# The denominator's product of a rational layer, on GpSimd from two magnitudes of ScalarE in place of VectorE from PSUM

## The chip, the core and the metric

The kernel runs on one core of one Trainium2 chip. The metric is the device time of one execution in microseconds, lower is better; the kernel before takes 723.6 us (median of three runs). A core has five engines that run their own instruction lists in order and wait for each other through semaphores: PE (TensorE, matrix products into PSUM), DVE (VectorE), ACT (ScalarE), POOL (GpSimd, which here reads and writes SBUF alone) and SP (which issues the DMAs).

## What is computed

Three stages follow each other. Attention with pooled queries gives `x` (1152 tokens by 512). The first layer puts a rational function between two matrix products, and the second layer is a gated one:

```python
h = x @ w_in                                  # 1152 x 2048
P = a[0] + a[1] * h + a[2] * h * h + a[3] * h * h * h
Q = 1.0 + np.abs(b[0]) * np.abs(h) + np.abs(b[1]) * h * h
g = P / (Q + 1e-06)
x = g @ w_out
...
silu = g * (1.0 / (1.0 + np.exp(-g)))         # second layer, g = xn @ w_gate
out = silu * (xn @ w_val) @ w_out
```

Only the first layer is touched. With u = |h|, the part of Q beyond 1 is (|b0| + |b1| u) u.

## The kernel before

Each product of the two layers is made from three passes (high by high, low by high, high by low part of the operands), so a block of 128 by 384 by 128 costs three matmuls. The 2048 hidden columns of the first layer are 16 **units** of 128; a unit's tile is 128 by 1152, in three parts of 384 tokens (`c`). PE makes a unit's `hid` tile (36 matmuls, lines 485 to 551) in one of two PSUM buffers. Units 0 and 1 are worked part by part (384 columns an instruction), the others whole (1152).

`rational` (line 1070) makes g from `hid`, and its steps are the names used below, with the unit behind them (p3_5 is p3 of unit 5):

- abs (L1106, ACT): `m_u` = |b1 h| from PSUM. p1 (L1109, ACT): `m_p` from PSUM. p2 (L1112, DVE) and p3 (L1115, DVE): the numerator's polynomial, each reads `m_p` and `hid`. p3 is the last to read `hid`, so it frees the PSUM buffer for the unit after next.
- q (L1122, DVE): `m_q` = (|b1 h| + |b0|) h, from `m_u` and PSUM. aq (L1125, ACT): its magnitude, which is the denominator's product.
- ln (L1128) and exp (L1134), ACT: the reciprocal of 1 + product, in `m_u`.
- One Newton step: q1 (L1131, ACT) and M (L1140, POOL) in even units, M (L1137, DVE) in odd ones.
- t (L1143, DVE), g (L1146, DVE): the quotient; both read SBUF alone. hi (L1154, ACT) and lo (L1157, POOL): its high and low part, which PE multiplies with `w_out`.

There are two buffers each of `m_u` and `m_q`, three of `m_p`, seven of `g_hi` and `g_lo`. `out1` (line 1193) sums g @ w_out over groups of units (0-1, 2-5, 6-9, 10-13, 14-15) in one of two PSUM buffers `accp`, and adds each finished block into `acc`: on ACT for the first group (L1210), on DVE for the others (L1212). Late in the layer the three instructions that turn a raw weight into fp32 (L176, L180, L186, DVE) and its split (L199, L204) stand between these steps.

What sets the order: every step is an `Op` with an engine, a cost by a formula (`cost`, line 428), a key and its buffers, and `order` (line 331) writes the engines' lists from these by a list schedule at build time. The costs know nothing of one engine that slows another. On the chip the lists are fixed, and every engine takes its own in order.

Of the kernel before, what the change touches and what calls it, by code (L numbers as in the profile page):

```python
# [11 lines left out]
AF = mybir.ActivationFunctionType  # L12
# [7 lines left out]
def attention_moe_moe2_kernel(  # L20
# [18 lines left out]
    nc = tc.nc  # L39
# [67 lines left out]
    b0, b1 = absb[:, 0:1], absb[:, 1:2]  # L107
# [204 lines left out]
            self.last = None  # L312

    ON_POOL = range(0, 16, 2)
    TOLL = {"DVE": 1.5, "ACT": 1.5}

    busy = {}
# [13 lines left out]
    def order(slack):  # L331
# [8 lines left out]
        def start(op):  # L340
# [5 lines left out]
            for way in op.ways:  # L346
                op.eng, op.cost, op.fn = way
                t = begin(op)
                w = t + op.cost * TOLL.get(op.eng, 1.0)
                if best is None or w < best[0]:  # L350
# [4 lines left out]
        def begin(op):  # L355
            e = op.eng
            if e not in op.data:
                op.data[e] = max((d.end + handoff(d.eng, e) for d in op.deps), default=0.0)
            t = max(busy.get(e, 0.0), op.data[e])
            if e == PE and op.mode != mode[0]:  # L360
                t = max(t, busy.get(e, 0.0) + SWITCH)
            for b in op.bufs:
                if b.last and b.last[0] != e:
                    t = max(t, b.last[1] + handoff(b.last[0], e))
                if not b.got:
                    m = made[b.tag]
                    if len(m) >= BUFS[b.tag]:
                        for eng, end in m[-BUFS[b.tag]].free.items():
                            t = max(t, end + handoff(eng, e) if eng != e else end)
            return t  # L370
# [55 lines left out]
    PE, DVE, ACT, POOL = "PE", "DVE", "ACT", "POOL"  # L426

    def cost(eng, n):
        return {PE: 0.45 * n, DVE: 100 + 1.09 * n, ACT: 165 + 0.85 * n, POOL: 180 + 2.15 * n}[eng]
# [53 lines left out]
    def project_ops(w, u, key, free=(), ps=None):  # L483
        ps = ps or Buf("hid")
        if w == "in" and u in FINE or w in ("gate", "val") and u == 0:
            parts = [(c, [kk]) for c in range(NC) for kk in range(KC)]
        else:
            parts = [(c, range(KC)) for c in range(NC)]
        done = {}
        for c, kks in parts:  # L490
            before = done.setdefault(c, [])
            before.append(Op(
                PE, cost(PE, 3 * len(kks) * CW), key + 1960 * c,
                lambda c=c, kks=kks: project(w, u, c, kks),
                [wop.get((w, u)), *free, *before[-1:], *xread.get((w, u, c), ()), *(o for kk in kks for o in xop.get((c, kk), ()))],
                [ps, *wbuf[w, u]],
            ))
        return ps, done
# [35 lines left out]
    def bank_access(w, u, c, ins):  # L534
        if w == "in" and u in FINE or (w, u) in (("gate", 0), ("val", NU2 - 1)):
            banked(hid_bank.setdefault((w, u), [[] for _ in range(NC)]), c, ins)
# [518 lines left out]
    def g_tile(x):  # L1055
        return T(f"g_{x}", [128, NTOK], F32R)

    def tmp(tag):
        return T(tag, [128, NTOK], F32)
# [10 lines left out]
    def rational(u, key):  # L1070


        ps, done = early_h.pop(u) if u in early_h else project_ops("in", u, key)
        k = key + 5900
        bu, bp, bq = (Buf(t) for t in ("m_u", "m_p", "m_q"))
        g = Buf("g_hi"), Buf("g_lo")
        gbuf[u] = g
        e = {}
        A = nc.scalar.activation
        stt = nc.vector.scalar_tensor_tensor  # L1080

        def part(tag, cs):
            if tag not in e:
                e[tag] = tmp(tag)
            return e[tag][:, cs[0] * CW:(cs[-1] + 1) * CW]

        def as3(t, cs):
            return t.rearrange("p (c n) -> p c n", c=len(cs))

        def chain(cs):  # L1090
            n = len(cs) * CW

            def u_():
                return part("m_u", cs)

            def p_():
                return part("m_p", cs)

            def q_():
                return part("m_q", cs)  # L1100

            def h_():
                return env["in", u][:, cs[0]:cs[-1] + 1, 0:CW]

            def f_abs():
                by_bank(A(as3(u_(), cs), h_(), AF.Abs, scale=b1))  # L1106

            def f_p1():
                by_bank(A(as3(p_(), cs), h_(), AF.Identity, bias=na2, scale=na3))  # L1109

            def f_p2():
                by_bank(nc.vector.tensor_mul(as3(p_(), cs), as3(p_(), cs), h_()))  # L1112

            def f_p3():
                by_bank(stt(as3(p_(), cs), as3(p_(), cs), na1, h_(), op0=ALU.add, op1=ALU.mult))  # L1115

            def by_bank(ins):
                if len(cs) == 1:
                    bank_access("in", u, cs[0], ins)

            def f_q():
                by_bank(stt(as3(q_(), cs), as3(u_(), cs), b0, h_(), op0=ALU.add, op1=ALU.mult))  # L1122

            def f_aq():
                A(q_(), q_(), AF.Abs)  # L1125

            def f_ln():
                A(u_(), q_(), AF.Ln, bias=b_lnq, scale=2.0**-62)  # L1128

            def f_q1():  # L1130
                A(q_(), q_(), AF.Identity, bias=b_one)  # L1131

            def f_exp():
                A(u_(), u_(), AF.Exp, bias=b_expq, scale=-1.0)  # L1134

            def f_m():
                stt(q_(), q_(), 1.0 + 1e-6, u_(), op0=ALU.add, op1=ALU.mult)  # L1137

            def f_m_pool():
                nc.gpsimd.tensor_mul(q_(), q_(), u_())  # L1140

            def f_t():
                stt(p_(), p_(), na0, u_(), op0=ALU.add, op1=ALU.mult)  # L1143

            def f_g():
                stt(p_(), q_(), 2.0, p_(), op0=ALU.subtract, op1=ALU.mult)  # L1146

            def g_(l):
                if ("g", u) not in env:
                    env["g", u] = [g_tile(x) for x in ("hi", "lo")]  # L1150
                return env["g", u][l][:, cs[0] * CW:(cs[-1] + 1) * CW]

            def f_hi():
                A(g_(0), p_(), AF.Copy)  # L1154

            def f_lo(eng=nc.gpsimd):
                eng.tensor_sub(g_(1), p_(), g_(0).bitcast(F32))  # L1157

            h = [o for c in cs for o in done.get(c, ())]
            o_abs = Op(ACT, cost(ACT, n), k, f_abs, h, [ps, bu])  # L1160
            o_p1 = Op(ACT, cost(ACT, n) + 165, k + 1000, f_p1, h, [ps, bp])
            o_p2 = Op(DVE, cost(DVE, n), k + 2200, f_p2, [o_p1], [ps, bp])
            o_p3 = Op(DVE, cost(DVE, n) + 60, k + 5500, f_p3, [o_p2], [ps, bp])
            o_q = Op(DVE, cost(DVE, n) + 60, k + 2000, f_q, [o_abs], [ps, bu, bq])
            o_aq = Op(ACT, cost(ACT, n), k + 2000, f_aq, [o_q], [bq])
            o_ln = Op(ACT, cost(ACT, n) + 110, k + 2000, f_ln, [o_aq], [bq, bu])
            o_exp = Op(ACT, cost(ACT, n) + 110, k + 8000, f_exp, [o_ln], [bu])
            if u in ON_POOL:
                o_q1 = Op(ACT, cost(ACT, n) + 100, k + 9000, f_q1, [o_ln], [bq])
                o_m = Op(POOL, cost(POOL, n), k + 3000, f_m_pool, [o_exp, o_q1], [bq, bu])  # L1170
            else:
                o_m = Op(DVE, 1.2 * cost(DVE, n), k + 7000, f_m, [o_exp], [bq, bu])
            o_t = Op(DVE, 1.3 * cost(DVE, n), k + 3000, f_t, [o_exp, o_p3], [bp, bu])
            o_g = Op(DVE, 1.3 * cost(DVE, n), k + 8700, f_g, [o_m, o_t], [bp, bq])
            o_hi = Op(ACT, cost(ACT, n), k + 5000, f_hi, [o_g], [bp, *g])
            o_lo = Op(POOL, cost(POOL, n), k + 5000, f_lo, [o_hi], [bp, *g], [(DVE, 1.3 * cost(DVE, n), lambda: f_lo(nc.vector))])
            for c in cs:
                gop[u, c] = o_lo
            env["table"] = o_exp

        for cs in [[c] for c in range(NC)] if u in FINE else [list(range(NC))]:
            chain(cs)
# [258 lines left out]
    def feed():  # L1441
# [28 lines left out]
        for g, t in zip(g2, y2):  # L1470
            out2(g, t, acc)
        TOLL.update({"DVE": 3})
        order(0)
# [33 lines left out]
```

## Time and profile before

| | us |
|---|---|
| median of 3 runs (721.89 to 726.38) | 723.6 |
| the profiled execution | 723.87 |
| its span, first to last instruction | 722.0 |
| PE busy in the span | 694.9 |
| DVE busy | 542.4 |
| ACT busy | 402.2 |
| POOL busy | 299.7 |

The profiled execution takes 1.87 us more than its span. Attention fills the span to about 265 us, the first layer to about 485, the norm and the second layer the rest. Busy time of a PE whose matmuls are pipelined hides nothing where it stands still: idle time there is what a change off PE can win.

### The profile page before, as it was taken

Reading aid. Unit: us, or ns where it says so; the run is one execution under the profiler, and the core shown is the slowest. Engines: PE = TensorE matmul, PEld = TensorE weight load, DVE = VectorE, ACT = ScalarE, POOL = GpSimd, SP = SyncE. Lnnn points to the kernel's source line nnn. Section 1 sums busy time; section 2 is a strip of 40 time slices with the busy share of each in tenths; the row PEclk is TensorE's granted clock in tenths of the full one; section 3 lists DMA queues with packets and bytes.
Section 4 is the critical chain, followed back from the end, with each engine's and each line's share of the span. In section 5 each row is a group of like instructions: output and inputs, shape, how many; then the busy total and the mean of one; then the engine's idle time right before and its main releaser. Section 6 shows DMA issues by size and latency. Waiting matters only on the chain.

```text
span 722.0 us, 13129 instructions
## 1 busy us (share of the span) xinstructions
PE 694.9 (96%) x5257; PEld 605.0 (84%) x5257; DVE 542.4 (75%) x706; ACT 402.2 (56%) x620; POOL 299.7 (42%) x275
## 2 busy tenths in 40 slices
PE   7899999999999998899899999999999999999997
PEld 6677677767776777799899999998999899989996
DVE  4699988988888876887977879957769146945844
ACT  4668768778777767888755766435333223302210
POOL 4035546565655664424432343435345033513400
PEclk9999999999999999899999999999999999999999
DMA  6424536356554426114104104010223212420103
GB/s 208 118 76 150 154 99 216 128 186 220 167 183 162 145 108 233 59 59 145 59 30 146 59 0 147 26 35 0 88 88 119 87 58 70 136 88 29 59 1 131
DMA packets 51596, 77.13 MB, mean 107 GB/s; under 512 B 4176, under 2 KB 33872, under 8 KB 51536
## 3 DMA queue, kind: packets, MB, share of 16 engines
q1 hardware_dynamic: 51536, 76.30, 32.6%
q8 instruction: 41, 0.67, 0.4%
q14 instruction: 19, 0.16, 0.1%
HBM read 61.87 MB, written 14.42 MB: 106 GB/s over the span
## 4 chain that ended last, share of the span: by engine, by line
PE 88%; DVE 4%; ACT 4%; issue 1%; DMA 1%; SPq 0%; POOL 0%; POOLq 0%; DVEq 0%; ACTq 0%
PE hid L507 33%; PE accp L507 23%; PE hid L764 11%; PE av L919 10%; PE hid L815 7%; PE prep L712 3%; ACT p L799 2%; DVE nm L793 2%; ACT pt L847 1%; PE prep L966 1%; DMA wout_lo<-far 1%; DMA qn<-in_q_dram 1%; DVE win_lo L204 0%; ACT m_u L1106 0%; ACT m_q L1125 0%
## 5 line engine op out<-in xcount | busy, mean ns | idle before, releaser
L507 PE MATMUL hid<-x_hi,win_hi 128*128 128x384 f32 x480 | 162.7, 339 | 5.3 <-issue 2.8
L507 PE MATMUL hid<-x_lo,win_hi 128*128 128x384 f32 x480 | 161.8, 337 | 0.0
L507 PE MATMUL hid<-x_hi,win_lo 128*128 128x384 f32 x480 | 161.4, 336 | 0.0
L799 ACT ACTIVATE p<-hid,nm 128x1152 f32<-128x1152 f32 x72 | 88.0, 1222 | 36.8 <-DVE nm L793 36.6
L793 DVE TENSOR_REDUCE nm<-hid 128x1 f32<-128x1152 f32 x72 | 95.1, 1353 | 9.5 <-PE hid L764 8.8
L764 PE MATMUL hid<-kT,qT 64*128 64x256 f32 (+3 forms) x800 | 98.1, 379 | 0.6 <-ACT qT L598 0.2
L507 PEld LDWEIGHTS hid<-x_hi,win_hi 128*128 128x128 f32 x480 | 91.0, 190 | 8.0 <-issue 5.6
L507 PEld LDWEIGHTS hid<-x_lo,win_hi 128*128 128x128 f32 x480 | 91.0, 190 | 1.3 <-DVE x_lo L1315 0.3
L507 PEld LDWEIGHTS hid<-x_hi,win_lo 128*128 128x128 f32 x480 | 90.9, 189 | 0.0
L764 PEld LDWEIGHTS hid<-kT,qT 64*128 64x128 f32 (+1 forms) x800 | 73.6, 180 | 11.7 <-issue 1.6
L815 PEld LDWEIGHTS hid<-ident,p 64*128 64x128 f32 x1296 | 53.1, 141 | 33.5 <-ACT p L799 14.6
L919 PE MATMUL av<-pt,vn 128*64 128x288 f32 x576 | 76.7, 411 | 0.0
L815 PE MATMUL hid<-ident,p 64*128 64x64 f32 x1296 | 66.8, 231 | 9.0 <-ACT p L799 7.8
L1157 POOL TENSOR_TENSOR g_lo<-m_p,g_hi 128x1152 fp32r<-128x1152 f32 (+1 forms) x20 | 44.1, 2211 | 69.4 <-ACT g_hi L1154 69.4
L847 ACT ACTIVATE pt<-hid 128x512 f32<-128x512 f32 (+2 forms) x127 | 56.0, 477 | 25.3 <-PE hid L815 24.3
L507 PE MATMUL accp<-g_hi,wout_hi 128*128 128x384 f32 x192 | 66.0, 344 | 4.2 <-DVE acc L1212 2.0
L199 POOL TENSOR_SCALAR win_hi<-wc 128x512 fp32r<-128x512 f32 x26 | 18.2, 698 | 123.0 <-PE hid L507 104.1
L171 ACT ACTIVATE wc<-wraw 128x512 f32<-128x512 f32 x68 | 45.8, 675 | 41.7 <-POOL wout_lo L204 19.5
L850 DVE COPY pt<-hid 128x512 f32<-128x512 f32 (+2 forms) x97 | 50.9, 541 | 22.6 <-PE hid L815 21.1
L507 PE MATMUL accp<-g_lo,wout_hi 128*128 128x384 f32 x192 | 65.8, 343 | 0.6 <-POOL g_lo L1157 0.6
L507 PE MATMUL accp<-g_hi,wout_lo 128*128 128x384 f32 x192 | 65.7, 342 | 0.0
L919 PEld LDWEIGHTS av<-pt,vn 128*64 128x64 f32 x576 | 38.6, 136 | 26.9 <-issue 2.8
(118 smaller groups left out, 1276.0 us busy)
## 6 DMA issues: line engine op xcount, KB each, us to landing
wraw<-in_moe_w_out_dram SPq DMA_DIRECT2D x28, 512.0 KB, 3.4
far<-spill SPq DMA_DIRECT2D x23, 512.0 KB, 3.2
wraw<-in_moe_w_in_dram SPq DMA_DIRECT2D x16, 512.0 KB, 4.0
wraw<-in_moe_w_gate_dram SPq DMA_DIRECT2D x12, 512.0 KB, 3.6
wraw<-in_moe_w_val_dram SPq DMA_DIRECT2D x12, 512.0 KB, 3.7
kn<-in_k_dram SPq DMA_DIRECT2D x16, 288.0 KB, 3.7
vn<-in_v_dram SPq DMA_DIRECT2D x16, 288.0 KB, 3.4
qn<-in_q_dram SPq DMA_DIRECT2D x16, 256.0 KB, 3.4
```

The source lines that it names most:

```text
L171: nc.scalar.activation(c.bitcast(F32), wt["raw", n][:, :, 1].bitcast(F32), AF.Abs, scale=2.0**-112)
L199: eng.tensor_scalar(hi, w_float(n), 1.0, 1.0, op0=ALU.mult, op1=ALU.mult)
L507: ins = nc.tensor.matmul(dst, lhsT=a[x], rhs=b[y], start=first and i == 0 and p == 0, stop=last and i == n - 1 and p == 2,)
L712: seen(nc.tensor.transpose(ps[0:src.shape[1], at:at + 128], src, ident))
L764: ins = nc.tensor.matmul(ps[to, j, c:c + x1 - x0], lhsT=qT[2 * pr + h][rows, c0:c0 + to.stop - to.start], rhs=kT[2 * pr + h][rows, x0:x1], ...
L793: nc.vector.tensor_reduce(out=e["nm"], in_=scores(), op=ALU.max, axis=AX.X, negate=True)
L799: nc.scalar.activation(e["p"], scores(), AF.Exp, bias=e["nm"], scale=1.0, accum_out=sums[pr][:, t:t + 1])
L815: ins = nc.tensor.transpose(ps[:, g, c:c + 64], e["p"][rows, 128 * j:128 * j + 128], ident[rows, rows])
L847: return nc.scalar.activation(to, src, AF.Copy)
L850: return nc.vector.tensor_copy(to, src)
L919: nc.tensor.matmul(e["av", h][64 * c:64 * c + 64, 0:QW], lhsT=v_tile[2 * pr + h][:, KEYS[kt], :], rhs=pt[pr, h][:, kt, c * QW:(c + 1) * QW ...
L1157: eng.tensor_sub(g_(1), p_(), g_(0).bitcast(F32))
```

## The change

`Q_POOL` holds all 16 units. ACT's abs writes u = |h| without the scale. A new ACT step, w (`f_w`), makes |b1| u + |b0| into `m_q`, and POOL (`f_qm`) multiplies it with u. That product is positive already, so both the DVE step q and the ACT step aq are gone. The names `o_w` and `o_aq` take their places in the list schedule.

```diff
+    Q_POOL = range(16)
...
             def f_abs():
-                by_bank(A(as3(u_(), cs), h_(), AF.Abs, scale=b1))
+                by_bank(A(as3(u_(), cs), h_(), AF.Abs, scale=1.0 if u in Q_POOL else b1))
+
+            def f_w():
+                A(q_(), u_(), AF.Identity, bias=b0, scale=b1)
+
+            def f_qm(eng):
+                eng.tensor_mul(q_(), q_(), u_())
...
-            o_q = Op(DVE, cost(DVE, n) + 60, k + 2000, f_q, [o_abs], [ps, bu, bq])
-            o_aq = Op(ACT, cost(ACT, n), k + 2000, f_aq, [o_q], [bq])
+            if u in Q_POOL:
+                o_w = Op(ACT, cost(ACT, n), k + 1500, f_w, [o_abs], [bu, bq])
+                o_aq = Op(POOL, cost(POOL, n), k + 2000, lambda: f_qm(nc.gpsimd), [o_w], [bu, bq])
+            else:
+                o_q = Op(DVE, cost(DVE, n) + 60, k + 2000, f_q, [o_abs], [ps, bu, bq])
+                o_aq = Op(ACT, cost(ACT, n), k + 2000, f_aq, [o_q], [bq])
```

The list schedule then comes out otherwise in the first layer, on PE, DVE, ACT and POOL. Attention, the norm and the second layer keep their order, and SP's list is the same throughout.

On POOL, from the last step of unit 2 to that of unit 5, the list before reads M2's successors like this (L1140 is M, L1157 is lo; the first row is lo2):

```order
L1157 TENSOR_TENSOR g_lo_4282<-m_p_4154,g_hi_4281 128x1152
L1157 TENSOR_TENSOR g_lo_4350<-m_p_4177,g_hi_4349 128x1152
L1140 TENSOR_TENSOR m_q_4312<-m_q_4312,m_u_4271 128x1152
L1157 TENSOR_TENSOR g_lo_4460<-m_p_4306,g_hi_4459 128x1152
L1157 TENSOR_TENSOR g_lo_4543<-m_p_4425,g_hi_4542 128x1152
```

Before, that is lo2, lo3, M4, lo4, lo5. In the changed kernel the lines stand lower in the file: L1113 is the new product (called qm below), L1147 is M, L1164 is lo.

```order
L1164 TENSOR_TENSOR g_lo_4283<-m_p_4157,g_hi_4282 128x1152
L1113 TENSOR_TENSOR m_q_4350<-m_q_4350,m_u_4266 128x1152
L1164 TENSOR_TENSOR g_lo_4396<-m_p_4233,g_hi_4395 128x1152
L1147 TENSOR_TENSOR m_q_4350<-m_q_4350,m_u_4266 128x1152
L1113 TENSOR_TENSOR m_q_4461<-m_q_4461,m_u_4444 128x1152
L1164 TENSOR_TENSOR g_lo_4482<-m_p_4325,g_hi_4481 128x1152
L1113 TENSOR_TENSOR m_q_4501<-m_q_4501,m_u_4472 128x1152
L1164 TENSOR_TENSOR g_lo_4570<-m_p_4447,g_hi_4569 128x1152
```

Now it is lo2, qm4, lo3, M4, qm5, lo4, qm6, lo5: a product of the next unit stands right behind M4.

On DVE, around the end of unit 4's and 5's polynomials, the list before has t4, q5, g4, p2_5, p3_5, t5, M5, q6, g5, p2_6, p3_6 (L1143 t, L1122 q, L1146 g, L1112 p2, L1115 p3, L1137 M):

```order
L1143 SCALAR_TENSOR_TENSOR m_p_4306<-m_p_4306,ncoef_83,m_u_4271 128x1152
L1122 SCALAR_TENSOR_TENSOR m_q_4427<-m_u_4419,absb_87,hid_4289 128x1152
L1146 SCALAR_TENSOR_TENSOR m_p_4306<-m_q_4312,m_p_4306 128x1152
L1112 TENSOR_TENSOR m_p_4425<-m_p_4425,hid_4289 128x1152
L1115 SCALAR_TENSOR_TENSOR m_p_4425<-m_p_4425,ncoef_83,hid_4289 128x1152
L1143 SCALAR_TENSOR_TENSOR m_p_4425<-m_p_4425,ncoef_83,m_u_4419 128x1152
L1137 SCALAR_TENSOR_TENSOR m_q_4427<-m_q_4427,m_u_4419 128x1152
L1122 SCALAR_TENSOR_TENSOR m_q_4514<-m_u_4483,absb_87,hid_4405 128x1152
L1146 SCALAR_TENSOR_TENSOR m_p_4425<-m_q_4427,m_p_4425 128x1152
L1112 TENSOR_TENSOR m_p_4499<-m_p_4499,hid_4405 128x1152
L1115 SCALAR_TENSOR_TENSOR m_p_4499<-m_p_4499,ncoef_83,hid_4405 128x1152
```

The q rows go, and the polynomials move. In the changed kernel (L1150 t, L1119 p2, L1153 g, L1122 p3) the same place reads: two weight instructions, t4, p2_5, g4, p3_5, p2_6, p3_6, t5.

```order
L180 SCALAR_TENSOR_TENSOR wc_4352<-wraw_3982,wc_4352 128x512
L186 SCALAR_TENSOR_TENSOR wc_4352<-wraw_3982,wc_4352 128x512
L1150 SCALAR_TENSOR_TENSOR m_p_4325<-m_p_4325,ncoef_83,m_u_4266 128x1152
L1119 TENSOR_TENSOR m_p_4447<-m_p_4447,hid_4300 128x1152
L1153 SCALAR_TENSOR_TENSOR m_p_4325<-m_q_4350,m_p_4325 128x1152
L1122 SCALAR_TENSOR_TENSOR m_p_4447<-m_p_4447,ncoef_83,hid_4300 128x1152
L1119 TENSOR_TENSOR m_p_4478<-m_p_4478,hid_4411 128x1152
L1122 SCALAR_TENSOR_TENSOR m_p_4478<-m_p_4478,ncoef_83,hid_4411 128x1152
L1150 SCALAR_TENSOR_TENSOR m_p_4447<-m_p_4447,ncoef_83,m_u_4444 128x1152
```

On PE, the new list has behind unit 5's projection 6 matmuls of `out1`, 36 of unit 6's projection, 6 of `out1`, 36 of unit 7's and 12 of unit 8's; before, it had 12 of `out1` between units 6 and 7.

p3_6 has moved ahead of t5 and g5; p3_5 still stands behind g4, and g4 behind p2_5.

## Rows read from the trace of the kernel before

**Rows 1.** The page's first part: busy us, share of the span, instructions.
```profile
PE 694.9 (96%) x5257; PEld 605.0 (84%) x5257; DVE 542.4 (75%) x706; ACT 402.2 (56%) x620; POOL 299.7 (42%) x275
```
**Rows 2.** Waits of PE, 281 to 310 us: us in total, times, longest.
```profile
PE hid L507 <- DVE m_p L1115: 1.9, 1, 1.9
PE accp L507 <- ACT g_hi L1154: 1.8, 1, 1.8
```
**Rows 3.** PE's timeline: start, us, what, idle before and its releaser.
```profile
349.44 0.41 PE L507 MATMUL hid<-x_hi,win_hi 128*128 128x384 f32 x1 [2.51 <-issue]
...
452.70 0.45 PE L507 MATMUL accp<-g_hi,wout_hi 128*128 128x384 f32 x1 [2.05 <-DVE acc L1212]
```
**Rows 4.** DVE's timeline, the columns of rows 3.
```profile
288.72 1.34 DVE L1146 SCALAR_TENSOR_TENSOR m_p<-m_q,m_p 128x384 f32<-128x384 f32 x1 [0.90 <-POOL m_q L1140]
...
339.97 2.79 DVE L1143 SCALAR_TENSOR_TENSOR m_p<-m_p,ncoef,m_u 128x1152 f32<-128x1152 f32 x1 [0.75 <-ACT m_u L1134]
...
347.92 1.42 DVE L1115 SCALAR_TENSOR_TENSOR m_p<-m_p,ncoef,hid 128x1152 f32<-128x1152 f32 x1
...
358.54 1.42 DVE L1115 SCALAR_TENSOR_TENSOR m_p<-m_p,ncoef,hid 128x1152 f32<-128x1152 f32 x1
...
371.55 1.42 DVE L1143 SCALAR_TENSOR_TENSOR m_p<-m_p,ncoef,m_u 128x1152 f32<-128x1152 f32 x1
...
439.38 0.68 DVE L180 SCALAR_TENSOR_TENSOR wc<-wraw,wc 128x512 uint32<-128x512 uint32 x1
```
**Rows 5.** Windows of 2 us: PE, PEld, DVE, ACT, POOL busy, PEclk, DMA share, GB/s.
```profile
304.00:306.00 2.00, 1.94 (x5) 1.46 (x5) 1.01 (x1) 2.00 (x3) 1.94 (x3) 0.50 0.04 14
348.00:350.00 2.00, 0.56 (x3) 0.60 (x4) 1.33 (x1) 2.00 (x3) 1.03 (x1) 1.00 0.24 93
454.00:456.00 2.00, 2.00 (x7) 2.00 (x7) 1.63 (x2) 1.97 (x3) 0.71 (x1) 0.50 0.00 0
```
**Rows 6.** Windows of 10 us, the columns of rows 5.
```profile
300.00:310.00 10.00, 7.18 (x24) 6.10 (x24) 8.40 (x9) 8.86 (x13) 2.94 (x3) 0.67 0.15 52
340.00:350.00 10.00, 7.49 (x43) 7.20 (x43) 9.30 (x6) 6.83 (x7) 2.57 (x2) 1.00 0.17 56
450.00:460.00 10.00, 7.95 (x37) 7.63 (x36) 8.85 (x10) 7.99 (x8) 4.85 (x2) 0.83 0.00 0
```
**Rows 7.** Groups by form: busy us, mean ns | idle before, releaser.
```profile
L1122 DVE SCALAR_TENSOR_TENSOR m_q<-m_u,absb,hid 128x1152 f32<-128x1152 f32 x14 | 19.7, 1409 | 12.4 <-ACT m_p L1109 11.4 <-ACT m_u L1106 0.9
L1146 DVE SCALAR_TENSOR_TENSOR m_p<-m_q,m_p 128x1152 f32<-128x1152 f32 x14 | 18.9, 1353 | 4.3 <-POOL m_q L1140 4.2
L1125 ACT ACTIVATE m_q<-m_q 128x1152 f32<-128x1152 f32 x14 | 16.4, 1169 | 10.7 <-DVE m_q L1122 10.6
L1131 ACT ACTIVATE m_q<-m_q,b_one 128x1152 f32<-128x1152 f32 x7 | 8.7, 1250 | 0.0
L1122 DVE SCALAR_TENSOR_TENSOR m_q<-m_u,absb,hid 128x384 f32<-128x384 f32 x6 | 3.7, 609 | 0.3 <-ACT m_p L1109 0.3
```
**Rows 8.** POOL's timeline, the columns of rows 3.
```profile
287.44 3.50 POOL L1140 TENSOR_TENSOR m_q<-m_q,m_u 128x384 f32<-128x384 f32 x3 [9.10 <-ACT m_q L1131]
...
325.71 2.70 POOL L1157 TENSOR_TENSOR g_lo<-m_p,g_hi 128x1152 fp32r<-128x1152 f32 x1 [3.82 <-ACT g_hi L1154]
...
338.87 2.68 POOL L1157 TENSOR_TENSOR g_lo<-m_p,g_hi 128x1152 fp32r<-128x1152 f32 x1 [5.12 <-ACT g_hi L1154]
...
351.60 3.79 POOL L1140 TENSOR_TENSOR m_q<-m_q,m_u 128x1152 f32<-128x1152 f32 x1
...
358.57 2.69 POOL L1157 TENSOR_TENSOR g_lo<-m_p,g_hi 128x1152 fp32r<-128x1152 f32 x1 [3.18 <-ACT g_hi L1154]
...
372.80 2.71 POOL L1140 TENSOR_TENSOR m_q<-m_q,m_u 128x1152 f32<-128x1152 f32 x1 [2.89 <-ACT m_q L1131]
```
**Rows 9.** The chain that ended last: start, us, what.
```profile
384.09 12.48 PE hid L507 x72
```
**Rows 10.** ACT's timeline, the columns of rows 3.
```profile
331.36 1.23 ACT L1106 ACTIVATE m_u<-hid,absb 128x1152 f32<-128x1152 f32 x1 [0.44 <-PE hid L507]
```

## The prediction

> **What bounds the kernel now.** I read the page's busy shares first: PE is busy for 694.9 of 722.0 us [rows 1], so only its idle time and its slow stretches can be won, and the change touches those of the first layer alone. Then PE's waits and timeline in that layer, from 265 to 485 us. Four matter. A: 1.9 us at 283 us, for p3 of unit 0, which frees `hid` for unit 2. C: 1.8 us before 303 us, for unit 1's g_hi [rows 2], with two shorter ones behind it: from 300 to 310 us PE idles 10.00 - 7.18 = 2.8 us [rows 6]. D: 2.51 us before 349.44; the profile says "issue", but p3_6 ends at 347.92 + 1.42 = 349.34 and the matmul wants its buffer [rows 3, 4]. E: 2.05 us before 452.70, for an add of DVE [rows 3]. Then the granted clock: it is 0.50, the lower of the two levels, after C and after E, but stays at 1.00 right after D, which was longer [rows 5]. Over ten microseconds the mean is 0.67 and 0.83 [rows 6], so C costs up to 3.3 us more and E 1.7 us. With the clock, C is about 6 us, D 2.5 and E 3.7: some 12 us that DVE, ACT and POOL answer for, besides A. In each of these stretches DVE is 84 to 93% busy [rows 6]: it is DVE's chain that PE waits for, and the change is aimed there.
>
> **What it removes and adds.** DVE loses q: 14 of 1.41 us and 6 of 0.61, 23.4 us [rows 7]. ACT loses aq, 14 of 1.17 us, and gains w, the form of q1 at 1.25 us: 14 x 0.08 = 1.1 us, hidden beside an ACT that is 56% busy [rows 1, 7]. POOL gains 14 products of 2.71 us and 6 of about 1.17 (3.50 / 3): 37.9 + 7.0 = 45 us [rows 8]. POOL's list has idle time for it [rows 1]. A unit's own path to g gets longer: q and aq were 1.41 + 1.17 = 2.6 us, w and qm are 1.25 + 2.71 = 4.0 us, so 1.4 us more, and PE has one group of other units' matmuls beside it; alone this costs nothing, from 0 to 1.4 us at the layer's end, where the last unit's g has no follower; there the 144 matmuls of units 10 to 13, 25 us at 12.48 / 72 a matmul [rows 9], still cover it. I take 0.
>
> **The price that the list schedule doesn't see.** DVE and POOL stop each other. t of unit 5 began at 339.97 and took 2.79 us, while lo4 ran on POOL from 338.87 to 341.55; alone t takes 1.42 (371.55) [rows 4, 8]. It stood until POOL's instruction was over, then did its work. It goes the other way too: M6 took 3.79 in place of 2.71 with a waiting t in front of it [rows 8]. But p3 at 358.54, which reads PSUM and one SBUF tile, took its usual 1.42 beside a lo of 2.69 [rows 4, 8]. So what reads two SBUF tiles on DVE (t, g, M, the weights' L180 and L186) is held by any POOL tensor instruction to its end, and what reads PSUM is not. The removed q is of the kind that is never held (1.409 us mean, like p3 [rows 7]), while the added qm holds t, g and M. So the change does not shift load between the two, it adds 45 us of holding.
>
> The Trainium skill (Perfetto Trace Analysis, section Optimizing Scalar/DVE Operations) says that offloading between GpSimd and DVE might not help, since they share an SBUF read port. Read as an exchange, that would be no gain and no loss, 723.9 us, the third rival below; the rows say that it is no exchange here, since q was never held.
>
> **Where it lands on PE.** Three places, walked with the durations above in the order of the changed lists.
> - Start. Stall A stays: p3 of unit 0 waits for ACT's p1 of its third part, which now stands behind w and ln of the first part, while four q's are gone from DVE; I get the same end within half a microsecond. C: unit 1's chain is earlier since DVE's two q's between the g's of unit 0 are gone, but g of unit 0 is held by POOL's products again (it was already: a third-size g took 1.34 us where M ran in a row of three [rows 4, 8]). I take 2 us of its 6 as won (bounds: 0.5 lost, 6 won).
> - Units 5 to 7, where PE's new list runs the projections of units 6, 7 and 8 almost back to back. D goes, as p3_6 now stands ahead of t5 and g5: -2.5 us (bounds -2.5 and 0). But p3_5 stands behind g4, which needs M4, and qm5 follows M4 on POOL at once, so it takes POOL's turn before g4 is released. Count from the end of unit 5's projection. In the trace lo3 started at 325.71, 5.6 us before unit 5's abs at 331.36, which PE released [rows 8, 10]; now a qm4 of 2.7 stands ahead of it and holds g3 for as long again, so I put it 1 us behind it. Then lo3 2.69, the two weight instructions and t4 that waited for it 0.68 + 0.68 + 1.42 = 2.8, M4 2.71, qm5 2.71, g4 1.35, p3_5 1.41 [rows 4, 7, 8]: 1 + 13.7 = 14.7 us. PE has 6 + 36 + 6 matmuls until it wants that buffer, 48 x 0.173 = 8.3 us [rows 9]. It waits 6.4 us. Bounds: 0, if M4 and the weights don't collide and qm5 is late (2.8 and 2.7 off leave 0.9), to 7.5, if POOL goes between the weights and t4. The nearest row is t's 2.79, which shows such a hold in full, so I take 6.4. One more of this kind, g2 behind M2 and qm3 ahead of p3_3, has more room: of its hold of 2.7 us I leave a little under half, 1.2 us, before unit 5 (0 to 2.7).
> - Units 8 to 15. Adds of DVE stand behind held t's and g's; a hold of 2.7 us exceeds the 2.1 us that one `accp` buffer's 12 matmuls give. E's own q15 and t14 give way to t14 behind qm15, with adds behind it. I take a third of E as won, 1.2 us (0 to 3.7), and as much lost elsewhere (0 to 5, two holds that reach PE in full).
>
> A wait of 6 us on PE would also bring the slow clock as E did: 1.7 us (0, as after D, to 3 x 1.7 for three such waits).
>
> Sum: -2.0 - 2.5 - 1.2 + 1.2 + 6.4 + 1.2 + 1.7 = +4.8 us on the profiled execution's 723.87 us, **728.7 us**; that execution stands 0.3 us above the median of the runs shown, so the base hardly matters.
>
> **Rivals.**
> 1. Relief wins (0.17). If the holds fall where PE has work, C, D and E go and nothing comes: 723.9 - 12.2 = 711.7 us at best; with half of C left, and one hold of 2.7 us on PE, 717. For it: DVE's 84 to 93% in the stretches of the stalls and 23.4 us off it. Against it: M and qm stand in a row on POOL by the list itself.
> 2. POOL's products hold DVE in every pair (0.25), which is the slower side: M is followed by the next unit's qm four times (M2, M4, M6, M8), so g is held 2.7 us four times, 10.8 us, and each hold that reaches PE brings 1.7 us of slow clock, 6.8 us. If all reach it and only C's 2 us, D and 1.2 us of E are won: 723.9 - 5.7 + 17.6 = 735.8 us. It decides once PE's lead on p3 and on the adds is under 2.7 us at these places; D and E in the trace show that it can be, the other units of the trace that PE waited at nothing.
> 3. Nothing changes (0.13). PE's work hides what is won and lost, or a lost hold equals a won stall: 722 to 726, at 723.9. For it: PE stands for 96%; against it, PE's own list moves in this layer, and the stalls named above are real.
>
> The forecast itself, 722 to 735 us around 728.7, has 0.45.
>
> **How the numbers follow.** What a measurement of this kernel can tell from no change is about 1%, 7.2 us: 716.4 and 730.8 are the lines. Faster by over 1% is over half of rival 1: 0.10. Slower is most of rival 2 (0.21) and the upper part of the forecast (0.17): 0.38. Within 1% is the rest, 0.52. The range leaves out the best of rival 1 (0.08) and the worst of rival 2, where adds and clock come on top (0.10): 715 to 742 us.
>
> **What would show it.** Right: POOL's busy time grows by 45 us and DVE's falls by less than 23.4, with t, g and M at means well above 1.42 and 1.35; D's wait before unit 8's projection is gone; PE waits several microseconds for p3_5 before unit 7's projection, with g4 held by qm5 just before it. Wrong: p3_5 in time, means of t and g as before, or PE's waits in the first layer under 6 us in sum. If those waits are the same in sum and the time still changes, the cause is elsewhere than I say.

## The result, and the profile after

The changed kernel takes 734.0 us, median of six runs (731.44 to 735.62); the kernel before took 723.8 us beside it. The ratio is 1.014 (95% interval 1.012 to 1.016), so it is 10.2 us slower. The forecast was 4.8 us slower. The page's first part shows where to look (busy us, share, instructions):

```profile
PE 697.8 (95%) x5257; PEld 606.1 (83%) x5257; DVE 542.5 (74%) x686; ACT 403.5 (55%) x620; POOL 350.0 (48%) x295
```

Beside [rows 1], POOL has 50.3 us more, and DVE has the same busy time to 0.1 us, although twenty q's with 23.4 us are gone from it. The groups by form in the first layer say what filled the gap (columns of [rows 7]):

```profile
L1150 DVE SCALAR_TENSOR_TENSOR m_p<-m_p,ncoef,m_u 128x1152 f32<-128x1152 f32 x14 | 27.6, 1970 | 4.1 <-ACT m_u L1141 3.9
L1153 DVE SCALAR_TENSOR_TENSOR m_p<-m_q,m_p 128x1152 f32<-128x1152 f32 x14 | 26.3, 1880 | 4.0 <-POOL m_q L1147 3.9
L1122 DVE SCALAR_TENSOR_TENSOR m_p<-m_p,ncoef,hid 128x1152 f32<-128x1152 f32 x14 | 19.7, 1407 | 1.8 <-ACT m_u L1107 1.6
...
L1113 POOL TENSOR_TENSOR m_q<-m_q,m_u 128x1152 f32<-128x1152 f32 x14 | 40.9, 2922 | 13.2 <-ACT m_q L1110 13.2
```

t (L1150) and g (L1153), which read two SBUF tiles, average 1.97 and 1.88 us; a g was 1.353 before [rows 7]. p3, which reads PSUM, stays at 1.41. The new product takes 2.92 us.

PE's timeline, with the start of the layer (the matmul that waits for attention's last ACT step), the waits over 1 us and the norm's transposition (idle before, and its releaser, in the brackets):

```profile
266.04 0.44 PE L508 MATMUL hid<-x_hi,win_hi 128*128 128x384 f32 x1 [0.37 <-ACT pt L848]
...
285.89 0.41 PE L508 MATMUL hid<-x_hi,win_hi 128*128 128x384 f32 x1 [1.65 <-DVE m_p L1122]
...
295.31 0.41 PE L508 MATMUL hid<-x_hi,win_hi 128*128 128x384 f32 x1 [1.87 <-issue]
...
317.62 0.41 PE L508 MATMUL hid<-x_hi,win_hi 128*128 128x384 f32 x1 [1.22 <-issue]
...
343.52 0.66 PE L508 MATMUL hid<-x_hi,win_hi 128*128 128x384 f32 x1 [6.55 <-issue]
...
374.80 0.44 PE L508 MATMUL accp<-g_hi,wout_hi 128*128 128x384 f32 x1 [1.82 <-DVE acc L1223]
...
427.06 0.69 PE L508 MATMUL accp<-g_hi,wout_hi 128*128 128x384 f32 x1 [2.57 <-DVE acc L1223]
...
477.74 0.44 PE L508 MATMUL accp<-g_hi,wout_hi 128*128 128x384 f32 x1 [1.09 <-DVE acc L1223]
...
504.70 0.54 PE L1310 MATMUL hid<-ident,small 128*128 128x128 f32 x3 [1.42 <-DVE small L1306]
```

C, D and E of [rows 2, 3] are gone; A is 1.65 us. In their place stand 6.55 us before unit 7's projection, 1.82 and 2.57 us for adds of DVE, and smaller ones. Between the same two instructions the layer took 228.58 us before and takes 238.66 now, 10.1 us more. This length, "the layer" below, is a finer measure than the whole time, since attention varies by some us from one execution to another (the layer starts at 263.29 us in run 1 and at 266.04 here). It comes from one execution of each kernel. Its PE row in the windows view (us, PE busy, granted clock, DMA share, GB/s) is first of before, then of after:

```profile
265.15:493.73 228.58, 217.54 (x1224) 0.97 0.24 79
```
```profile
266.04:504.70 238.66, 219.10 (x1224) 0.97 0.23 76
```

So 8.5 of the 10.1 us are idle time (11.04 to 19.56) and 1.6 are more busy time. The slow stretches moved, as windows of 10 us show (columns of [rows 6]). The first is of before and shows a slow stretch behind A, beside those of [rows 6]; in the changed kernel this window has a clock of 1.00. The others are of after:

```profile
280.00:290.00 10.00, 8.08 (x38) 7.79 (x37) 8.78 (x17) 9.00 (x18) 2.56 (x3) 0.83 0.76 264
```
```profile
300.00:310.00 10.00, 9.71 (x55) 9.10 (x54) 6.79 (x8) 9.44 (x13) 6.26 (x5) 1.00 0.16 52
340.00:350.00 10.00, 6.48 (x25) 6.51 (x26) 9.23 (x7) 7.98 (x7) 5.28 (x2) 0.66 0.05 18
370.00:380.00 10.00, 8.18 (x39) 7.86 (x38) 8.03 (x7) 4.83 (x4) 5.78 (x3) 0.83 0.01 2
420.00:430.00 10.00, 7.43 (x35) 7.11 (x35) 9.85 (x8) 4.66 (x4) 6.72 (x3) 0.84 0.00 0
```

In sum the slow clock took no more than before. From windows of 2 us, the time in which PE was busy, times the share of the clock that was missing, is 1.7 us behind A, 2.9 behind C and 1.7 behind E before, 6.3 in all; after, it is 2.4, 1.7 and 1.6 behind the waits that end at 343.52, 374.80 and 427.06, 5.6 in all.

In front of the waits DVE and POOL run like this. First DVE's timeline, then POOL's (start, us):

```profile
312.39 3.80 DVE L1153 SCALAR_TENSOR_TENSOR m_p<-m_q,m_p 128x1152 f32<-128x1152 f32 x1 [0.22 <-POOL m_q L1147]
...
329.72 3.06 DVE L180 SCALAR_TENSOR_TENSOR wc<-wraw,wc 128x512 uint32<-128x512 uint32 x1
332.81 3.05 DVE L186 SCALAR_TENSOR_TENSOR wc<-wraw,wc 128x512 uint32<-128x512 uint32 x1
335.78 3.79 DVE L1150 SCALAR_TENSOR_TENSOR m_p<-m_p,ncoef,m_u 128x1152 f32<-128x1152 f32 x1
339.49 1.34 DVE L1119 TENSOR_TENSOR m_p<-m_p,hid 128x1152 f32<-128x1152 f32 x1
340.75 1.34 DVE L1153 SCALAR_TENSOR_TENSOR m_p<-m_q,m_p 128x1152 f32<-128x1152 f32 x1
342.02 1.40 DVE L1122 SCALAR_TENSOR_TENSOR m_p<-m_p,ncoef,hid 128x1152 f32<-128x1152 f32 x1
...
370.45 3.83 DVE L1144 SCALAR_TENSOR_TENSOR m_q<-m_q,m_u 128x1152 f32<-128x1152 f32 x1
374.20 0.54 DVE L1223 TENSOR_TENSOR acc<-acc,accp 128x384 f32<-128x384 f32 x1
...
421.91 3.36 DVE L1153 SCALAR_TENSOR_TENSOR m_p<-m_q,m_p 128x1152 f32<-128x1152 f32 x1
```
```profile
312.30 2.68 POOL L1113 TENSOR_TENSOR m_q<-m_q,m_u 128x1152 f32<-128x1152 f32 x1
...
329.31 2.92 POOL L1164 TENSOR_TENSOR g_lo<-m_p,g_hi 128x1152 fp32r<-128x1152 f32 x1 [2.50 <-ACT g_hi L1161]
332.19 3.12 POOL L1147 TENSOR_TENSOR m_q<-m_q,m_u 128x1152 f32<-128x1152 f32 x1
335.27 3.08 POOL L1113 TENSOR_TENSOR m_q<-m_q,m_u 128x1152 f32<-128x1152 f32 x1
...
369.28 3.79 POOL L1113 TENSOR_TENSOR m_q<-m_q,m_u 128x1152 f32<-128x1152 f32 x1
...
420.27 3.79 POOL L1113 TENSOR_TENSOR m_q<-m_q,m_u 128x1152 f32<-128x1152 f32 x1
```

For the wait that ends at 343.52, lo3 holds L180, M4 holds L186, qm5 holds t4: each DVE instruction stands for one whole POOL instruction and then does its 0.68 to 1.42 us of work. p3_5 ends at 343.42, and PE goes on at 343.52. The other waits have holds in front of them too: qm3 (312.30) holds g2, with p3_3 and the wait that ends at 317.62 behind it; qm8 (369.28) holds M7, and the add behind M7 is the one PE waits for at 374.80; qm12 (420.27) holds g11, in front of the add that ends the wait at 427.06.

### The profile page after: what moved, and what is told of

Same layout as the page of the kernel before. It is cut to its first block, busy times and chain, and to the rows that moved or that the text cites. A ratio compares the mean times of both kernels' runs of the same rounds, so it can differ in the third digit from the quotient of the medians.

```text
span 732.7 us, 13116 instructions
## 1 busy us (share of the span) xinstructions
PE 697.8 (95%) x5257; PEld 606.1 (83%) x5257; DVE 542.5 (74%) x686; ACT 403.5 (55%) x620; POOL 350.0 (48%) x295
## 4 chain that ended last, share of the span: by engine, by line
PE 80%; DVE 9%; ACT 5%; POOL 2%; issue 2%; DMA 0%; SPq 0%; DVEq 0%; POOLq 0%; ACTq 0%
PE hid L508 30%; PE accp L508 18%; PE hid L765 11%; PE av L920 10%; PE hid L816 7%; PE prep L713 3%; ACT p L800 2%; DVE nm L794 1%; DVE m_q L1144 1%; DVE m_p L1150 1%; ACT pt L848 1%; DVE acc L1223 1%; POOL m_q L1147 1%; POOL m_q L1113 1%; DVE m_p L1153 1%
## 5 line engine op out<-in xcount | busy, mean ns | idle before, releaser
L1164 POOL TENSOR_TENSOR g_lo<-m_p,g_hi 128x1152 fp32r<-128x1152 f32 (+1 forms) x20 | 45.4, 2275 | 49.3 <-ACT g_hi L1161 49.3
```

## The experiments

The theory: what the change loses is DVE's time in such holds, by the new product's time on POOL. The rivals: the product's own length in each unit's chain and in POOL's queue; the new order of the lists, on PE above all; ACT's w. Ratios are to the kernel before on the same chip. In all but the seventh and the eighth run the lists of PE, DVE and ACT keep the order of the kernel that the run starts from.

**1. The product on 64 columns.**

```diff
-                eng.tensor_mul(q_(), q_(), u_())
+                m = slice(0, 64 if True else None)
+                eng.tensor_mul(q_()[:, m], q_()[:, m], u_()[:, m])
```

> The changed kernel with every engine's list as it is, but POOL's new product works on 64 of a unit's 1152 (or 384) columns, so the denominator is wrong in the rest: POOL's new work is nearly gone, and the rest of the change (q and aq gone, w on ACT, PE's new order) stays. If the product's time on POOL is the cause (its holds of DVE, or its own length in the chain): DVE busy falls from 542.5 to about 518 us, t and g come back to means of about 1.7 and 1.4 us from 1.97 and 1.88, PE's wait before unit 7's projection falls from 6.55 us to under 2 and the waits at 374 and 427 us go: 714 to 719 us. If the new order of the lists or ACT's longer w is the cause: 730 to 734 us with the same waits on PE.

Measured: 712.7 us, ratio 0.9875 (0.9843 to 0.9906). DVE busy falls to 521.5 us. PE's timeline:

```profile
263.29 0.44 PE L508 MATMUL hid<-x_hi,win_hi 128*128 128x384 f32 x1 [0.37 <-ACT pt L848]
...
333.11 0.41 PE L508 MATMUL hid<-x_hi,win_hi 128*128 128x384 f32 x1 [1.78 <-issue]
...
482.82 0.54 PE L1311 MATMUL hid<-ident,small 128*128 128x128 f32 x3 [1.41 <-DVE small L1307]
```

The layer is 219.53 us: without the product's time the rest of the change gains 9.1 us, and the product costs 238.66 - 219.53 = 19.1. The new lists and w are not the cause. The granted clock is 1.00 throughout this layer: the 6.3 us of slow clock that the kernel before has are most of the gain.

**2. The product of unit 5 alone on 64 columns.**

```diff
-                eng.tensor_mul(q_(), q_(), u_())
+                m = slice(0, 64 if u == 5 else None)
+                eng.tensor_mul(q_()[:, m], q_()[:, m], u_()[:, m])
```

> The changed kernel with the same lists, but the product of unit 5 alone works on 64 of 1152 columns. If t4 was held by qm5: t4 falls from 3.79 to about 1.4 us and PE's wait before unit 7's projection from 6.55 to about 4 us; with the slow stretch behind it a little shorter, 730 to 732 us. If the wait comes from the order of p3_5 behind g4 and not from the hold: the wait stays above 6 us, 734 us.

Measured: 730.2 us, 1.0102 (1.0076 to 1.0127). t4 takes 1.47 us in place of 3.79, and the wait before unit 7's projection is 4.24 us. The layer is 234.33 us, 4.3 us shorter than the changed kernel's. Of this, 2.3 us are this wait and 0.7 the slow stretch behind it; most of the rest, 1.6 us, is the slow stretch behind the wait of 2.57 us before 423.89, which doesn't come here, although that wait is as long as in the changed kernel. So the hold of t4 is one part of that wait, worth about 3 us, and between two single executions a slow stretch alone can make 1.6 us. The holds by lo3 and M4 remained.

**3. The kernel before with an idle instruction on POOL.** It reads `m_q` and a spare tile and writes the spare tile.

```diff
             def f_ln():
+                m = part("spare", cs)
+                nc.gpsimd.tensor_sub(m, q_(), m)
                 A(u_(), q_(), AF.Ln, bias=b_lnq, scale=2.0**-62)
```

> The kernel before with all lists as they are on PE, DVE, ACT and SP, and with a POOL instruction put in beside each aq that reads m_q and a spare tile, writes the spare tile and whose result nobody uses: 14 of 1152 columns and 6 of 384. No chain gets longer but by its turn on POOL. If DVE is held by POOL's instructions: DVE busy rises from 542.4 by 15 to 30 us, t and g rise from 1.76 and 1.35 us to about 2.0 and 1.9, and the time rises by 8 to 20 us, 732 to 744 us. If POOL's product costs through its length in the unit's own chain and not through DVE: DVE busy within 5 us of 542.4 and 722 to 727 us.

Measured: 733.4 us, 1.0144 (1.0120 to 1.0169), as much as the changed kernel, with a layer of 238.40 us. DVE busy is 560.0 us, 17.6 more than before, in the groups that read two SBUF tiles:

```profile
L1147 DVE SCALAR_TENSOR_TENSOR m_p<-m_p,ncoef,m_u 128x1152 f32<-128x1152 f32 x14 | 30.6, 2185 | 1.9 <-ACT m_u L1138 1.8
L1150 DVE SCALAR_TENSOR_TENSOR m_p<-m_q,m_p 128x1152 f32<-128x1152 f32 x14 | 26.3, 1877 | 6.0 <-POOL m_q L1144 6.0
L1117 DVE SCALAR_TENSOR_TENSOR m_p<-m_p,ncoef,hid 128x1152 f32<-128x1152 f32 x14 | 19.7, 1407 | 0.1
...
L1131 POOL TENSOR_TENSOR spare<-m_q,spare 128x1152 f32<-128x1152 f32 x14 | 38.6, 2761 | 22.5 <-ACT m_q L1127 22.5
```

Nobody waits for this result, so the product's length in a unit's own chain isn't needed for the loss. POOL's queue (M and lo start later) was not excluded by this run; run 5 does that.

**4. POOL's instructions in thirds**, qm as shown, M and lo likewise.

```diff
-                eng.tensor_mul(q_(), q_(), u_())
+                for c in cs:
+                    eng.tensor_mul(part("m_q", [c]), part("m_q", [c]), part("m_u", [c]))
```

> The changed kernel with the same lists, but each 1152-column instruction of POOL in the rational function (qm, M, lo) is written as three of 384 columns. The result is the same. If DVE is held to the end of one POOL instruction, a hold is at most 1.1 us in place of 2.9: t, g, M and the weights' instructions fall to means under 1.7 us and 1.3 us, DVE busy to under 530 us, PE's wait before unit 7's projection to under 4 us: 721 to 728 us. If a hold depends on how much POOL has queued and not on the length of one instruction: means as in the changed kernel, and with POOL's 10 us of added fixed cost 734 to 738 us.

Measured: 729.8 us, 1.0097 (1.0067 to 1.0127), layer 234.56 us. Half a hit. DVE busy falls to 524.0 us, t to 1.67 us and both weight instructions to under 1.1, but the product now takes 61.2 us on POOL (48 of 1300 ns) in place of 47.4, and PE's wait is 4.82 us: g4 stood for M4 itself, which ended late behind a longer lo3. Shorter POOL instructions mean shorter holds; here POOL's own time, 25.2 us more in all where I had put 10, took most of it back.

**5. POOL as busy, but with memsets.**

```diff
-                eng.tensor_mul(q_(), q_(), u_())
+                eng.tensor_mul(q_()[:, 0:64], q_()[:, 0:64], u_()[:, 0:64])
+                for _ in range(2):
+                    eng.memset(q_()[:, 64:], 0.5)
```

> As the run with the product on 64 columns (same lists), but behind those POOL fills the other columns of m_q with a constant, twice, so the denominator there is a constant: two memsets of about 1 us each, so POOL is busy and ln waits for it almost as long as for the whole product (about 2.5 in place of 2.9 us), but POOL reads no tensor in them. If the time is lost by DVE's holds, and a memset does not hold: t and g at means as in the 64-column run (1.7 and 1.5 us) and 712 to 719 us. If it is lost by POOL's own queue (lo, M and ln behind the product): 728 to 734 us with t and g short. If a memset holds DVE as a product does: 728 to 734 us with t and g near 1.9 us.

Measured: 715.7 us, 0.9890 (0.9858 to 0.9921); POOL busy 342.5 us, DVE 522.6:

```profile
L1152 DVE SCALAR_TENSOR_TENSOR m_p<-m_p,ncoef,m_u 128x1152 f32<-128x1152 f32 x14 | 22.5, 1611 | 6.9 <-ACT m_u L1143 6.9
L1155 DVE SCALAR_TENSOR_TENSOR m_p<-m_q,m_p 128x1152 f32<-128x1152 f32 x14 | 20.8, 1488 | 4.4 <-POOL m_q L1149 4.3
...
L1115 POOL MEMSET m_q<- 128x1088 f32 x28 | 28.5, 1019 | 0.8
```

POOL's queue and ln's wait are nearly those of the changed kernel (2.34 us in place of 2.92 for a unit), but t and g are short and the loss is gone. This parts the hold from the queue: the hold is the cause. The layer is 222.39 us, so 16.3 of the 19.1 us are holds and what follows from them, and 2.9 are left for a queue a fifth shorter; of these, 1.7 are a slow stretch behind a wait of 1.77 us before 335.86, which came in run 1 as well (1.78 us) without one. The Trainium skill (SBUF — State Buffer, section Who interferes with whom) says that a DVE instruction with two SBUF inputs contends with a GpSimd instruction that reads SBUF and not with one that only writes it; these rows agree.

**6. The products of units 8 and 12 alone on 64 columns.**

```diff
-                eng.tensor_mul(q_(), q_(), u_())
+                m = slice(0, 64 if u in (8, 12) else None)
+                eng.tensor_mul(q_()[:, m], q_()[:, m], u_()[:, m])
```

> The changed kernel with the same lists, but the products of units 8 and 12 alone work on 64 of 1152 columns. If the adds that PE waits for at 374 and 427 us are late because M7 is held by qm8 and g11 by qm12: both waits (1.82 and 2.57 us) go or fall under 0.5 us, the clock stays at its upper level behind them, 725 to 728 us. If the adds are late by the order of the lists: 733 to 734 us.

Measured: 726.6 us, 1.0033 (1.0014 to 1.0053), layer 231.60 us. M7 takes 1.47 us in place of 3.83 and g11 1.34 in place of 3.36; the wait at 375 us is gone, the one at 427 us is 0.56 us, and the granted clock is 1.00 in every 10 us behind 350. Two products of twenty were worth 7.1 us of the layer: 1.82 and 2.0 us of waits, the rest slow clock (in run 2 one of these two slow stretches stayed away by itself).

**7. M of the even units back on DVE.**

```diff
-    ON_POOL = range(0, 16, 2)
+    ON_POOL = ()
```

> The changed kernel with M of the even units on DVE too, as in the odd units (q1 goes), so POOL has the product and lo alone; the lists are made anew. POOL's new work is then 45 less 24 us and no product stands behind an M. If all of POOL's two-tensor time holds DVE, in step with its amount: 722 to 728 us. If the harm is in the row M, then product: 714 to 719 us. If the holds do not matter and DVE's load does: DVE gains about 13 us of M, 735 us or more.

Measured: 724.4 us, 0.9997 (0.9978 to 1.0017), no change from before. POOL is at 327.3 us, and the layer is 229.53 us. That fits a loss that goes with the amount of POOL's work on two tiles, but the lists were made anew and DVE has the M's of eight more units, so this run alone doesn't show it. Holds don't need a product right behind an M: g still averages 1.72 and M 2.01 us.

**8. The denominator from ACT alone**, by a square: neither POOL nor DVE has the product. `sqc` holds s, c, and the constants 1 + 1e-6 - c c for q1, M and ln. It needs a b1 that isn't near zero, or c c swallows the digits of the rest.

```diff
-                A(q_(), u_(), AF.Identity, bias=b0, scale=b1)
+                A(q_(), u_(), AF.Square, bias=sqc[:, 1:2], scale=sqc[:, 0:1])
...
-                o_w = Op(ACT, cost(ACT, n), k + 1500, f_w, [o_abs], [bu, bq])
-                o_aq = Op(POOL, cost(POOL, n), k + 2000, lambda: f_qm(nc.gpsimd), [o_w], [bu, bq])
+                o_aq = Op(ACT, cost(ACT, n), k + 2000, f_sq, [o_abs], [bu, bq])
```

> The denominator from ACT alone: |b1| u u + |b0| u = (s u + c) squared, less c squared, with s the root of |b1| and c = |b0| / (2 s); ACT's Square takes the place of w, and neither POOL nor DVE has a product. ln, q1 and M take the constant 1 - c c. DVE loses q's 23.4 us and POOL gains nothing, ACT keeps two steps as before; the lists are made anew. If POOL's holds are what the change lost by: 710 to 717 us, below both kernels. If PE waits in the first layer for other chains whatever DVE's load: 720 to 726 us.

Measured: 724.6 us, 1.0018 (0.9999 to 1.0036). A miss. In the lists made anew p3_6, which frees the buffer for unit 8, stands behind t5, M5 and g5, as in the kernel before, and behind two weight instructions ahead of them, and PE waits 4.98 us before 350.75 us. POOL instructions that were there before the change hold two of these:

```profile
338.51 3.06 DVE L188 SCALAR_TENSOR_TENSOR wc<-wraw,wc 128x512 uint32<-128x512 uint32 x1
...
346.13 3.19 DVE L1158 SCALAR_TENSOR_TENSOR m_p<-m_q,m_p 128x1152 f32<-128x1152 f32 x1
...
349.24 1.40 DVE L1127 SCALAR_TENSOR_TENSOR m_p<-m_p,ncoef,hid 128x1152 f32<-128x1152 f32 x1
```

lo and M of POOL (338.09 to 341.01, and 345.49 to 348.11) stand beside the first two, which take 0.68 and 1.35 us alone: 4.2 us of hold ahead of p3_6. The relief of DVE was there, and the list schedule, which knows no hold, spent it. That the order spent it, and not the square, is what run 9 shows.

**9. The same square in the changed kernel's lists**: the schedule still counts a POOL product, but nothing is issued for it.

```diff
-                o_aq = Op(POOL, cost(POOL, n), k + 2000, lambda: f_qm(nc.gpsimd), [o_w], [bu, bq])
+                o_aq = Op(POOL, cost(POOL, n), k + 2000, lambda: None, [o_w], [bu, bq])
```

> The squared denominator on ACT as in the run before, but with the changed kernel's lists: Square stands where w stood, and POOL's product is left out of its list with nothing in its place; ln waits for ACT alone. If the run with new lists lost by how they came out (the projections of units 6 to 8 in a row): PE's wait before unit 7's projection is 1.5 to 2 us as in the 64-column run, and the time 711 to 715 us. If Square or the constants cost something of their own: 720 us or more.

Measured: 716.9 us, 0.9915 (0.9883 to 0.9947); faster than both kernels, and nothing of the computation is left out. Square stands where w stood. The layer is 219.46 us, as in run 1, and the granted clock is 1.00 throughout it. So the order of the lists made 229.27 - 219.46 = 9.8 us between runs 8 and 9.

**10. The square in the lists of before**: q left out, nothing moved.

```diff
-                by_bank(stt(as3(q_(), cs), as3(u_(), cs), b0, h_(), op0=ALU.add, op1=ALU.mult))
+                q_()
...
-                A(q_(), q_(), AF.Abs)
+                A(q_(), u_(), AF.Square, bias=sqc[:, 1:2], scale=sqc[:, 0:1])
```

> The squared denominator with the lists of the kernel before: q is left out of DVE's list with nothing in its place, and Square stands where aq stood. This is DVE's relief by 23.4 us with no new order on PE and no new work on POOL. If relief alone makes the gain: C, D and E go or shrink, 710 to 716 us. If the gain of the 64-column run needs the new lists: 718 to 723 us.

Measured: 722.8 us, 0.9978 (0.9953 to 1.0003). D is gone and E falls to 0.70 us, but C stays at 1.68 us, with the clock at 0.83 from 290 to 320 us. The layer is 225.96 us, 2.6 less than before. Relief of DVE alone is worth little; the gain of run 9 (9.1 us of the layer) needs it together with the changed kernel's lists.

**11. Run 9 with M and lo in thirds**, M as shown, lo likewise.

```diff
-                nc.gpsimd.tensor_mul(q_(), q_(), u_())
+                for c in cs:
+                    nc.gpsimd.tensor_mul(part("m_q", [c]), part("m_q", [c]), part("m_u", [c]))
```

> As the squared denominator with the changed kernel's lists, with M and lo on POOL written as three instructions of 384 columns each. If a shorter POOL instruction means a shorter hold: t and the weights' instructions shorten, PE's wait before unit 7's projection goes from near 1.8 us to under 1, and the time is 0 to 3 us under that run. If POOL's own longer time counts for more, as lo and M then end about 1 us later each: 1 to 4 us over it.

Measured: 714.9 us, 0.9906 (0.9871 to 0.9941). The median is lower than in run 9, but the layer is 220.21 us, not shorter, and the wait before unit 7's projection is 2.25 us. t falls to 1.57 us, and POOL has 13 us more. A slow stretch behind that wait, which run 9 has not, is 1.7 us of this. No gain in the layer is shown.

## Why the prediction was off by half

The direction, the mechanism and the main place were right; one term, the loss in units 8 to 15, was sized far too small, and another, the win at the start, erred the other way.

- **Holds, not exchange.** "it adds 45 us of holding" was right in kind. The products took 47.4 us of POOL, and 21 us of them show as holds in DVE's busy time (542.5 against 521.5 in run 1). The product's time costs 19.1 us of the layer (run 1), some 16 of them by holds (run 5). Rival 3's exchange and rival 1's relief fall; but rival 1's prices, 711.7 and 717, are near what runs 1 and 9 reach (712.7 and 716.9) once the new product holds nothing. The Trainium skill (Perfetto Trace Analysis, section Optimizing Scalar/DVE Operations) says that such an offload might not help; here it cost more than twice what the rest of the change gained.
- **Before unit 7's projection.** Forecast 6.4 us, measured 6.55. It came about a little otherwise: I let qm5 hold g4, and instead lo3, M4 and qm5 held L180, L186 and t4 in turn. That was the upper bound's case ("if POOL goes between the weights and t4"). p2_5, 1.34 us between t4 and g4, wasn't in my sum. So that the two numbers agree this well is in part luck.
- **Before unit 5**, forecast 1.2, measured 1.22 us, and g2 was held by qm3 as I had it; the share of the hold that reached PE was a guess. D, forecast -2.5, is gone.
- **Start.** Forecast -2.0, measured -5.9. The window from 300 to 310 us has 0.29 us of idle time in place of 2.82, and a clock of 1.00 in place of 0.67. I priced that clock at 3.3 us, but part of the slow stretch was idle time already; it took 2.9. The prediction missed that the clock fell behind A too: 1.7 us, which are gone, and A is 0.3 us shorter. Against this, 1.87 us before 295.31 stand where before there was a wait of 0.34. Why the clock stays up behind A now is not shown.
- **Units 8 to 15: the step that failed.** "I take a third of E as won, 1.2 us (0 to 3.7), and as much lost elsewhere (0 to 5, two holds that reach PE in full)" gave nothing net. Measured: E's 2.05 us of wait go, and 1.82, 2.57 and three short ones of 1.86 us in sum come (1.09 at 477.74 the longest). With the clock, 3.3 us behind the two long ones less E's 1.7, that is 5.8 us lost where I had 0. Two holds reached PE nearly in full, and each brought its slow stretch. Run 6 shows the price of these two: 7.1 us. I had seen that a hold of 2.7 us exceeds the 2.1 us of one `accp` buffer, and then took less than half of one hold.
- **The clock.** Forecast 1.7 us behind one wait of 6 us. Behind the wait of 6.55 us it took 2.4, and 1.7 and 1.6 behind the two of units 8 to 15, 5.6 us in all, more than the bound of 3 x 1.7. But the 6.3 us of A, C and E went, so the clock is no part of the net loss.
- **The sum.** -5.9 - 2.5 + 1.2 + 6.55 + 2.4 + 5.8 = 7.6 us, and the layer grew by 10.1. The other 2.5 us had no term: waits under 0.2 us, and time on both sides of each wait, of which there are more now. Around D before, for example, two matmuls started 2.85 us apart (346.59 and 349.44) with 2.51 us of idle time, where 0.17 us is the usual distance.
- **Rival 2**, at 735.8 us, came nearer in number. But its four rows of M and qm did not all reach PE: M2 with 1.2 us and M4 did, M6 and M8 did not. The other two waits came from a product behind a lo (lo6 with qm8, lo10 with qm12), which it didn't name.

## What to carry to other kernels

Before an operation is moved from VectorE to GpSimd, ask which operands it has: one that read PSUM and one SBUF tile was not held in any of these runs (p3 at 1.41 us in all of them), and its replacement on GpSimd held VectorE instructions that read two SBUF tiles, so relief and price are not the same microseconds. To size it, where both queues are full, count each VectorE instruction of that kind as held for one whole GpSimd instruction, and price what reaches PE with the slow clock that may stand behind it. And after a change of costs look at what the list schedule made of it: the same arithmetic took 9.8 us more or less of this layer by the order alone.

## What the runs showed that was not expected

- **The turns alternate.** In the stretch from 329 to 340 us, with both queues full, neither engine got two turns in a row: L180, L186 and t4 each stood for one POOL instruction (2.92, 3.12, 3.08 us), while POOL lost no more than the other's work: 3.12 in place of 2.7 beside a weight instruction of 0.68, and later 3.79 (qm8) beside an instruction of 1.42. The one with the shorter instructions paid.
- **A memset of POOL held nothing** (run 5): 1019 ns for 1088 columns, with g4 beside it at 1.46 us.
- **The slow clock.** It followed waits of 1.82 and 2.57 us at 375 and 427 us, and A's 1.92 us in the kernel before, but not those of 1.87 and 1.22 us before 320 us, nor D's 2.51 us [rows 5], nor the same 2.57 us in run 2. The length of the wait alone doesn't say; what does was not tried.
